# Halved span loads and 64x64 state products in a linear-attention plus gated-MLP kernel

## The chip, the cores and the metric

The kernel runs on one core of a Trainium2 chip. The core has a matrix engine (TensorE, in the profile PE, with its weight loads as PEld), a vector engine (VectorE, DVE), an activation engine (ScalarE, ACT), a general-purpose engine (GpSimd, POOL) and a queue engine (SyncE, SP) that issues DMA transfers. GpSimd issues DMA transfers too. The metric is the device time of one execution in microseconds; the median of three runs is 202.58 us (202.42 to 202.94).

## The reference, cut to what matters

Two stages are computed one after the other. The first is linear attention with a decay per head, in blocks of 64 positions; 4 batches, 8 heads, 768 positions, head size 64:

```
for b in range(12):
    intra = einsum('bhic,bhjc->bhij', qb, kb) * Dmask      # lam ** (i - j) for i >= j
    intra = einsum('bhij,bhjd->bhid', intra, vb)
    inter = einsum('bhid,bhde->bhie', qb * lam_pow, kv_state)
    out[block b] = intra + inter
    kv_state = lam_block * kv_state + einsum('bhsd,bhse->bhde', kb * rev_pow, vb)
```

The second is a gated MLP on the 3072 rows of 512 numbers that the attention gives: h = x @ w_in (512 to 2048), g = h * cos(h), result g @ w_out (2048 to 512). Inputs and result are float32; the matrix products of the kernel are in bfloat16.

## The kernel before, in words

The work is cut into 24 blocks of 128 positions, and these into MLP tiles of 4, 2, 2, 2, 2, 2, 2, 4 and 4 blocks. An MLP tile takes the transposed attention output xT, multiplies it by 16 column chunks of w_in (L732), turns each into g on ScalarE (cos, L738) and VectorE (product, L744), and multiplies g by w_out in groups of four chunks (L778). ScalarE copies the result out (L792), and SyncE stores it.

The first four blocks are two "spans" (`add_span`, x = 0 and 1) of 256 positions each, one for each of the first two batches. In a span a row of the tile holds two neighbouring positions. For each span SyncE loads q and k (512 KB each, all 8 heads at once), and GpSimd loads v. q and k are scaled by head halves hp = 0 and 1 (L593: VectorE, but GpSimd for k of the second span), transposed on TensorE (L601), copied by ScalarE (L604), multiplied to scores (L612) and masked on VectorE (L617). Then come the values (L638), the state of the span's first half (`update`, L625), its copies into kv_bd (L629), the part of the output that comes from that state (`carried`, L644), and the copies into xT (L652) from which the first MLP tile starts. In `update` a product takes two heads at once: 64 positions, a 128-wide k and a 128-wide v, so that of each 128x128 result only the two 64x64 blocks on the diagonal are used.

The later blocks are handled in pairs: `prepare` scales q (L329), k (L333) and v (L337) and transposes; `add_scores` and `add_stretch` compute scores, state and values in 64x64 products. For the first pair (blocks 4 and 5) the first q is scaled on VectorE and the second on GpSimd. From block 6 on the transposes are DMA transposes.

The order of the instructions on every engine is not written by hand. A small planner (`Planner.order`) plays the tasks through with a length, a latency and a priority for each, and gives the order in which they are issued. So a changed length or latency in the code moves other instructions too. Where the plan leaves TensorE without work in the lead-in, `keep_awake` puts in filler matmuls (L866, L870) of the planned length.

The loads stand in a list of their own: `ORDER` (L36) gives the first ones, and the loop at L817 the dependencies. The first pair's q waits for the MLP's first tile to be nearly through its gate (`pace`), v4 waits for k4 to have landed, and the last quarter of w_out (o3) waits for q4. Chunks of w_in and w_out are converted to bfloat16 by the DMA, issued on GpSimd.

Of the kernel before, what the change touches and what calls it, by code (L numbers as in the profile page):

```python
# [18 lines left out]
SPANS = 2  # L19
# [6 lines left out]
LOAD_US = 1.22  # L26
# [118 lines left out]
def kernel(  # L145
# [10 lines left out]
    nc = tc.nc  # L156
    B, H, S, D = q.shape
    P = 128
# [68 lines left out]
    pl = Planner({**BUFS, "q_f": BUFS["ld"], "k_f": BUFS["ld"], "v_f": BUFS["ld"]})  # L227
# [3 lines left out]
    halves = [slice(i * D, (i + 1) * D) for i in range(2)]  # L231
# [9 lines left out]
    load_t, issue_t = {}, {}  # L241
# [15 lines left out]
        return i  # L257

    def add_span_load(name, src, x, prio, deps):
        def emit(_):  # L260
            if on_pool:
                t = span_v[x]
            else:
                if ("raw", x) not in live:
                    live["raw", x] = work.tile([P, 2, H, 2, D], F32, tag="g", name="sp_f")
                t = live[name, "sp", x] = live["raw", x][:, "qk".index(name[0])]
            return start(nc.gpsimd if on_pool else nc.sync, t.rearrange("u h s d -> u h (s d)"),
                         src[x, :, 0:2 * P, :].rearrange("h (u s) d -> u h (s d)", s=2), deps)

        on_pool = name == "v_f"  # L270
        issue, load_t[name, "sp", x] = dma("POOL" if on_pool else "SP", 1.5, 1.0 if on_pool else 0.5, emit, prio, deps,
                                           lat=0.95 if on_pool else 1.0)
        return load_t[name, "sp", x]

    def add_load(n, name, src, prio, deps=()):
        b, c = where(n)

        def emit(_):
            t = loads.tile([P, H, D], F32, tag=name, name=name)
            live[name, n] = t  # L280
            i = start(nc.sync, t, src[b, :, c * P:(c + 1) * P, :].transpose([1, 0, 2]), deps)
            if (name, n) == ("q_f", 2 * SPANS):

                tc.add_manual_dep(i.ins, pace[0].ins.ins.name, mybir.DependencyInfo(
                    mybir.DependencyClass.Sync, mybir.DependencyReason.DATA), reason="order of loads")
            return i

        issue_t[name, n], load_t[name, n] = dma("SP", LOAD_US, 0.85, emit, prio, deps, get=name,
                                                lat=1.9 if name == "v_f" and n < 2 * SPANS + 2 else 1.0)
        return load_t[name, n]  # L290

    w_t, pace = {}, []
# [22 lines left out]
    def prepare(pr):  # L315
# [24 lines left out]
        a, k_ = [], []  # L340
        for s in range(2):
            n = 2 * pr + s
            eq = "DVE" if early and s == 0 else "POOL"
            ev = "DVE" if early and s == 1 else "POOL"
            a.append(pl.add(eq, us[eq], [load_t["q_f", n]] + a, partial(prep_q, s=s, e=eq), pa(-0.9), get=None if s else "qk"))
            k_.append(pl.add("ACT" if early else "POOL", 0.61, [load_t["k_f", n]] + ([] if early else [a[0]]), partial(prep_k, s=s), pa(-0.9)))
            d_t[n] = v_head[n] = pl.add(ev, us[ev], [load_t["v_f", n]], partial(prep_v, s=s, e=ev), pa(-0.85), get="v_s")
            for name, t in (("q_f", a[s]), ("k_f", k_[s]), ("v_f", d_t[n])):
                issue_t[name, n].frees = [t]
# [229 lines left out]
    def add_span(x):  # L579
# [40 lines left out]
        def update(t):  # L620
            L["kv"] = bank(t.bank[0], [P, NP, P], F32, "ps_kv")
            rows = chunks[0][0]
            for p in range(NP):
                for s in range(2):
                    nc.tensor.matmul(L["kv"][:, p, :], lhsT=L["k"][rows, s, 2 * p:2 * p + 2, :], rhs=L["v"][rows, s, 2 * p:2 * p + 2, :],  # L625
                                     start=(p == 0 and s == 0), stop=True, skip_group_check=True)

        def update_out(_, h, e):
            (nc.scalar.copy if e == "ACT" else nc.vector.tensor_copy)(kv_bd[h, x, :, h], L["kv"][h, :, h])  # L629
# [23 lines left out]
                live["xT", 0][:, :, n * P:(n + 1) * P], L["o"][c])  # L653

        s_first = None
        so, kt, v_t = [[], []], [], [load_t["v_f", "sp", x]]
        for hp in range(2):
            eq, ek = QK[x]["q"][hp], QK[x]["k"][hp]
            a = pl.add(eq, us[eq], [load_t["q_f", "sp", x]], partial(prep, name="q", hp=hp, e=eq), pa(-0.9 + 0.1 * hp))
            kt.append(pl.add(ek, us[ek], [load_t["k_f", "sp", x]], partial(prep, name="k", hp=hp, e=ek), pa(-0.9 + 0.1 * hp)))  # L660
            if x:
                w_t["in", 2].issue.deps.append(kt[hp])
            outs = []
            for name, src in (("qT", a), ("kT", kt[hp])):
                e = OUTS[x][name][hp]
                t = pl.add("PE", MM(P, 4), [src, s_first if name == "kT" else None], partial(transposes, name=name, hp=hp), pa(-0.5 + 0.1 * hp), banks=1)
                outs.append(pl.add(e, 0.58 if e == "ACT" else 0.42, [t], partial(transposes_out, name=name, hp=hp, e=e), pa(-0.5 + 0.1 * hp)))
                t.bank_frees = [[outs[-1]]]
            s1 = pl.add("PE", 0.42, outs, partial(scores, hp=hp), pa(0.1 + 0.1 * hp), banks=2)
            if x and hp == 0:  # L670
                s_first = s1
            so[hp] = [pl.add("DVE", 0.69, [s1], partial(scores_out, hp=hp, i=i), pa(0.1 + 0.1 * hp + 0.05 * i)) for i in range(2)]
            s1.bank_frees = [[t] for t in so[hp]]

        u = pl.add("PE", 0.42, v_t + kt + [spans[0].get("carried")], update, pv(0.1), banks=1)
        Uo_sp[x] = [pl.add(e, 0.4 if e == "ACT" else 0.42, [u], partial(update_out, h=h, e=e), pv(0.1))
                    for h, e in zip(halves, STATE_OUT[x])]
        u.bank_frees = [Uo_sp[x]]
        span_deps.extend(v_t + kt)
        v0 = pl.add("PE", 0.35, so[0] + v_t + [spans[0].get("carried")], partial(values, hp=0), pv(0.2), banks=2)  # L680
        v1 = pl.add("PE", 0.35, [v0] + so[1], partial(values, hp=1), pv(0.25))
# [249 lines left out]
```

## Time and profile before

| what | value |
|---|---|
| median of 3 runs | 202.58 us |
| the profiled execution's own time | 202.54 us |
| span of its instructions | 200.8 us |
| TensorE busy | 195.9 us (98%) |
| VectorE, ScalarE, GpSimd busy | 116.3, 119.4, 64.9 us |
| TensorE clock granted | 0.998 |
| q, k, v loads of a pair, median to landing | 3.9, 4.2, 5.1 us |

The span counts from the first to the last profiled instruction; the execution's own time is 1.7 us longer. A busy time of TensorE counts waiting inside its pipeline too, so 98% doesn't say that it is at its peak. Times in the timeline are from the span's start. A group's line gives the engine, the kernel line, what is written and read, and how often.

### The profile page before, as it was taken

How to read it: one execution, taken by the hardware profiler on the slowest of the kernel's cores; microseconds unless marked ns; L12 is line 12 of the kernel's file. 1: busy time of each engine (PE TensorE's matmuls, PEld its weight loads, DVE VectorE, ACT ScalarE, POOL GpSimd, SP SyncE). 2: the span in 40 equal slices, each digit the busy share in tenths (PEclk: the TensorE clock that was granted, in tenths of full speed). 3: DMA queues.
4: the chain of work that ended last, by engine and by line, in shares of the span. 5: the costliest groups of instructions: out<-in, count | busy, mean ns of one | idle time of the engine just before them, and what ended most of it. 6: DMA issues, size and time to landing. Idle time of an engine off the chain costs nothing.

```text
span 200.8 us, 5951 instructions
## 1 busy us (share of the span) xinstructions
PE 195.9 (98%) x2473; PEld 116.8 (58%) x2473; DVE 116.3 (58%) x230; ACT 119.4 (59%) x241; POOL 64.9 (32%) x85
## 2 busy tenths in 40 slices
PE   6999999999999999999999999999999999999994
PEld 3477444558757757766658676755445544444452
DVE  3978771269756948758458575835588354444001
ACT  4878771149658768666639666644887564345120
POOL 5893003085235360635555353545500000000000
PEclk9999999999999999999999999999999999999999
DMA  5999999999889997999999899979910010111112
GB/s 163 303 190 204 203 199 216 209 238 225 200 197 225 262 202 177 239 179 253 189 275 245 188 207 194 277 141 261 243 23 3 3 52 0 52 55 52 52 52 104
DMA packets 96620, 33.93 MB, mean 169 GB/s; under 512 B 84690, under 2 KB 93650, under 8 KB 96594
## 3 DMA queue, kind: packets, MB, share of 16 engines
q1 hardware_dynamic: 89088, 28.78, 63.2%
q0 software_dynamic: 7360, 4.72, 16.4%
q8 instruction: 19, 0.31, 0.7%
q10 hardware_dynamic: 146, 0.07, 0.1%
q14 instruction: 7, 0.06, 0.1%
HBM read 27.26 MB, written 6.29 MB: 167 GB/s over the span
## 4 chain that ended last, share of the span: by engine, by line
PE 95%; DMA 2%; ACT 0%; DVE 0%; SPq 0%; issue 0%; ACTq 0%; DVEq 0%
PE ps_h L732 42%; PE ps_f L778 42%; DMA sp_f<-in_k_dram 2%; PE ps_s L407 2%; PE ps_o L502 2%; PE ps_o L470 2%; PE ps_kv L419 1%; PE ps_t L601 1%; PE ps_s L612 1%; PE ps_o L638 1%; PE ps_kv L625 1%; PE ps_x L470 0%; PE ps_idle L870 0%; PE ps_t L359 0%; DVE k_sp L593 0%; PE ps_o L644 0%
## 5 line engine op out<-in xcount | busy, mean ns | idle before, releaser
L744 DVE TENSOR_TENSOR g<-ps_h,cos 128x256 bf16<-128x256 f32 (+1 forms) x149 | 73.1, 501 | 42.0 <-ACT cos L738 41.1
L738 ACT ACTIVATE cos<-ps_h,halfpi 128x256 f32<-128x256 f32 (+1 forms) x149 | 75.9, 536 | 29.3 <-PE ps_h L732 28.2
L778 PE MATMUL ps_f<-w_out_sb,g 128*128 128x512 bf16 (+2 forms) x400 | 91.4, 371 | 0.0
L732 PE MATMUL ps_h<-xT,w_in_sb 128*128 128x256 bf16 (+1 forms) x596 | 91.1, 303 | 0.0
L732 PEld LDWEIGHTS <-w_in_sb 128*128 128x128 bf16 x596 | 57.5, 98 | 30.1 <-DVE xT L510 0.4
L778 PEld LDWEIGHTS <-g 128*128 128x128 bf16 x400 | 37.6, 98 | 37.2
L329 POOL TENSOR_TENSOR qk<-q_f,q_scale 128x512 bf16<-128x512 f32 x19 | 20.0, 1067 | 34.7 <-DMA q_f<-in_q_dram 17.6
L792 ACT COPY o_sb<-ps_f 128x512 f32<-128x512 f32 (+1 forms) x24 | 13.7, 572 | 24.7 <-PE ps_f L778 24.5
L337 POOL TENSOR_TENSOR v_s<-v_f,v_scale 128x512 bf16<-128x512 f32 x19 | 19.6, 1042 | 9.8 <-DMA v_f<-in_v_dram 5.2
L412 DVE TENSOR_TENSOR s_m<-ps_s,mask 128x512 bf16<-128x512 f32 x20 | 13.0, 685 | 4.2 <-PE ps_s L407 3.6
L333 POOL CAST qk<-k_f 128x512 bf16<-128x512 f32 x18 | 11.0, 611 | 10.4 <-DMA k_f<-in_k_dram 10.2
L510 ACT CAST xT<-ps_o 128x512 bf16<-128x512 f32 x11 | 6.0, 588 | 9.0 <-PE ps_o L502 5.6
L425 DVE TENSOR_TENSOR sum<-sum,ps_kv 128x512 f32<-128x512 f32 x15 | 10.2, 682 | 0.6
L430 ACT CAST S<-sum 128x512 bf16<-128x512 f32 x15 | 9.1, 616 | 0.9 <-DVE sum L425 0.8
L253 POOL DMA_DIRECT2D w_out_sb<-in_moe_w_out_dram x4 | 3.0, 784 | 15.8 <-DMA q_f<-in_q_dram 15.8
L792 DVE COPY o_sb<-ps_f 128x384 f32<-128x384 f32 x1 | 0.6, 557 | 11.6 <-DMA out_dram<-o_sb 11.6
L470 PEld LDWEIGHTS <-v_s 64*64 64x64 bf16 x320 | 4.0, 107 | 4.2 <-issue 3.4
L870 PE MATMUL ps_idle<-blank 128*128 128x512 f32 (+2 forms) x8 | 4.7, 707 | 1.7 <-DVE blank L215 1.7
L487 DVE COPY spare<-ps_o 1x1 f32<-1x1 f32 x6 | 0.9, 156 | 8.4 <-PE ps_o L470 8.4
L617 DVE TENSOR_TENSOR s_m_sp<-ps_s,mask_sp 128x512 bf16<-128x512 f32 x8 | 5.1, 684 | 1.2 <-PE ps_s L612 1.2
L470 PE MATMUL ps_o<-s_m,v_s 64*64 64x64 bf16 x256 | 5.2, 196 | 0.0
L502 PE MATMUL ps_o<-qkT,S 64*64 64x64 bf16 x304 | 4.9, 195 | 0.0
(76 smaller groups left out, 90.1 us busy)
## 6 DMA issues: line engine op xcount, KB each, us to landing
q_f<-in_q_dram SPq DMA_DIRECT2D x20, 256.0 KB, 3.9
k_f<-in_k_dram SPq DMA_DIRECT2D x20, 256.0 KB, 4.2
v_f<-in_v_dram SPq DMA_DIRECT2D x20, 256.0 KB, 5.1
out_dram<-o_sb SPq DMA_DIRECT2D x19, 256.0 KB, 2.5
w_out_sb<-in_moe_w_out_dram POOLq DMA_DIRECT2D x4, 512.0 KB, 12.4
sp_f<-in_q_dram SPq DMA_DIRECT2D x2, 512.0 KB, 4.9
sp_f<-in_k_dram SPq DMA_DIRECT2D x2, 512.0 KB, 5.5
w_in_sb<-in_moe_w_in_dram POOLq DMA_DIRECT2D x2, 512.0 KB, 8.9
```

Of the source, the lines that this page charges most:

```text
L329: vec[e].tensor_mul(new_qk()[:, 0, :, s], live.pop(("q_f", 2 * pr + s)), q_scale[:, c, :].unsqueeze(2).to_broadcast([P, H, D]))
L333: (nc.scalar.copy if early else nc.gpsimd.tensor_copy)(new_qk()[:, 1, :, s], live.pop(("k_f", 2 * pr + s)))
L337: vec[e].tensor_mul(live["v_s", 2 * pr + s], live.pop(("v_f", 2 * pr + s)), v_scale[:, c, :].unsqueeze(2).to_broadcast([P, H, D]))
L412: nc.vector.tensor_mul(t, live["s", pr][s], mask.unsqueeze(1).to_broadcast([P, H, D]))
L425: nc.vector.tensor_add(new, live["sum", pr, 0] if half else live["sum", pr - 1, 1], live["kv", pr][half])
L430: nc.scalar.copy(new_S(pr, half), live["sum", pr, half])
L470: yield lambda h=h: nc.tensor.matmul(o[halves[h % 2], h // 2], lhsT=live["v_s", n0 + s][m, h, :], rhs=live["s_m", n0 + s][m, h, :], start= ...
L732: nc.tensor.matmul(t[:, :n], lhsT=w_in_sb[:, kd, f * P:(f + 1) * P], rhs=live["xT", i][:, kd, at], start=(kd == 0), stop=(kd == KD - 1))
L738: nc.scalar.activation(c[:, :n], live["h", i, f, at.start][:, :n], AF.Sin, bias=halfpi)
L744: return nc.vector.tensor_mul(live["g", i][:, f, at], live.pop(("h", i, f, at.start))[:, :n], live.pop(("c", i, f, at.start))[:, :n])
L778: nc.tensor.matmul(live["f", i, j, piece][:, :width], lhsT=live["g", i][:, f, j * P:(j + 1) * P], rhs=w_out_sb[:, f, part], start=(f == 0) ...
L792: (nc.scalar.copy if eng == "ACT" else nc.vector.tensor_copy)(o[:, :width], live["f", i, j, piece][:, :width])
```

## The change

- `add_span_load` issues the load of a span's q or k as two loads, one for each half of the heads, each planned at half the length and with a latency of 0.7 us where it was 1.0. The scaling of a head half depends on its own half alone. v is loaded whole as before.
- In the plan, the first pair's loads get 1.0 us each (they had 1.22), and their v a latency of 2.7 us (it had 1.9). v4 no longer depends on the landing of k4.
- The first pair's second q is scaled on VectorE.
- `update` of a span makes its state in 16 products on 64x64 blocks where it had 8 on 64x128, two heads' blocks for each head pair and each of the two positions of a row.
- The planned lengths of a span's scores, update and values are changed to 0.32, 0.3 and 0.3 us.

The planner's order on all engines follows from these numbers. The built order differs in the lead-in on TensorE, ScalarE and VectorE, in SyncE's queue of loads, stores and DMA transposes, and in the places where small attention products stand between the MLP's groups.

```
     def add_span_load(name, src, x, prio, deps):
-        def emit(_):
+        on_pool = name == "v_f"
+        cuts = [slice(0, H)] if on_pool else [slice(0, H // 2), slice(H // 2, H)]
+
+        def emit(_, cut):
...
-            return start(nc.gpsimd if on_pool else nc.sync, t.rearrange("u h s d -> u h (s d)"),
-                         src[x, :, 0:2 * P, :].rearrange("h (u s) d -> u h (s d)", s=2), deps)
...
-        issue, load_t[name, "sp", x] = dma("POOL" if on_pool else "SP", 1.5, 1.0 if on_pool else 0.5, emit, prio, deps,
-                                           lat=0.95 if on_pool else 1.0)
-        return load_t[name, "sp", x]
+            return start(nc.gpsimd if on_pool else nc.sync, t[:, cut].rearrange("u h s d -> u h (s d)"),
+                         src[x, cut, 0:2 * P, :].rearrange("h (u s) d -> u h (s d)", s=2), deps)
+
+        parts = [dma("POOL" if on_pool else "SP", 1.5 / len(cuts), 1.0 if on_pool else 0.5, partial(emit, cut=cut), prio, deps,
+                     lat=0.95 if on_pool else 0.7)[1] for cut in cuts]
+        load_t[name, "sp", x] = parts if len(parts) > 1 else 2 * parts
+        return parts[-1]
...
-        issue_t[name, n], load_t[name, n] = dma("SP", LOAD_US, 0.85, emit, prio, deps, get=name,
-                                                lat=1.9 if name == "v_f" and n < 2 * SPANS + 2 else 1.0)
+        issue_t[name, n], load_t[name, n] = dma("SP", 1.0 if n < 2 * SPANS + 2 else LOAD_US, 0.85, emit, prio, deps, get=name,
+                                                lat=2.7 if name == "v_f" and n < 2 * SPANS + 2 else 1.0)
...
-            eq = "DVE" if early and s == 0 else "POOL"
+            eq = "DVE" if early else "POOL"
...
-                    nc.tensor.matmul(L["kv"][:, p, :], lhsT=L["k"][rows, s, 2 * p:2 * p + 2, :], rhs=L["v"][rows, s, 2 * p:2 * p + 2, :],
-                                     start=(p == 0 and s == 0), stop=True, skip_group_check=True)
+                    for i, h in enumerate(halves):
+                        nc.tensor.matmul(L["kv"][h, p, h], lhsT=L["k"][rows, s, 2 * p + i, :], rhs=L["v"][rows, s, 2 * p + i, :],
+                                         start=(p == 0 and s == 0), stop=True, skip_group_check=True)
...
-            a = pl.add(eq, us[eq], [load_t["q_f", "sp", x]], partial(prep, name="q", hp=hp, e=eq), pa(-0.9 + 0.1 * hp))
-            kt.append(pl.add(ek, us[ek], [load_t["k_f", "sp", x]], partial(prep, name="k", hp=hp, e=ek), pa(-0.9 + 0.1 * hp)))
+            a = pl.add(eq, us[eq], [load_t["q_f", "sp", x][hp]], partial(prep, name="q", hp=hp, e=eq), pa(-0.9 + 0.1 * hp))
+            kt.append(pl.add(ek, us[ek], [load_t["k_f", "sp", x][hp]], partial(prep, name="k", hp=hp, e=ek), pa(-0.9 + 0.1 * hp)))
...
-            s1 = pl.add("PE", 0.42, outs, partial(scores, hp=hp), pa(0.1 + 0.1 * hp), banks=2)
+            s1 = pl.add("PE", 0.32, outs, partial(scores, hp=hp), pa(0.1 + 0.1 * hp), banks=2)
...
-        u = pl.add("PE", 0.42, v_t + kt + [spans[0].get("carried")], update, pv(0.1), banks=1)
+        u = pl.add("PE", 0.3, v_t + kt + [spans[0].get("carried")], update, pv(0.1), banks=1)
...
-        if name == f"v{2 * SPANS}":
-            deps = [load_t["k_f", 2 * SPANS]]
+        if name in (f"v{2 * SPANS}", f"v{2 * SPANS + 1}"):
+            deps = []
```

More of the change, by code (lines that the diff above doesn't have):

```diff
@@ L266, in emit @@
                 t = live[name, "sp", x] = live["raw", x][:, "qk".index(name[0])]
-            return start(nc.gpsimd if on_pool else nc.sync, t.rearrange("u h s d -> u h (s d)"),
-                         src[x, :, 0:2 * P, :].rearrange("h (u s) d -> u h (s d)", s=2), deps)
-        on_pool = name == "v_f"
-        issue, load_t[name, "sp", x] = dma("POOL" if on_pool else "SP", 1.5, 1.0 if on_pool else 0.5, emit, prio, deps,
-                                           lat=0.95 if on_pool else 1.0)
-        return load_t[name, "sp", x]
+            return start(nc.gpsimd if on_pool else nc.sync, t[:, cut].rearrange("u h s d -> u h (s d)"),
[4 more added lines that the diff above has]
+        return parts[-1]
     def add_load(n, name, src, prio, deps=()):
@@ L655, in add_span @@
         s_first = None
-        so, kt, v_t = [[], []], [], [load_t["v_f", "sp", x]]
+        so, kt, v_t = [[], []], [], [load_t["v_f", "sp", x][0]]
         for hp in range(2):
             eq, ek = QK[x]["q"][hp], QK[x]["k"][hp]
-            a = pl.add(eq, us[eq], [load_t["q_f", "sp", x]], partial(prep, name="q", hp=hp, e=eq), pa(-0.9 + 0.1 * hp))
-            kt.append(pl.add(ek, us[ek], [load_t["k_f", "sp", x]], partial(prep, name="k", hp=hp, e=ek), pa(-0.9 + 0.1 * hp)))
+            a = pl.add(eq, us[eq], [load_t["q_f", "sp", x][hp]], partial(prep, name="q", hp=hp, e=eq), pa(-0.9 + 0.1 * hp))
+            kt.append(pl.add(ek, us[ek], [load_t["k_f", "sp", x][hp]], partial(prep, name="k", hp=hp, e=ek), pa(-0.9 + 0.1 * hp)))
             if x:
@@ L679, in add_span @@
         span_deps.extend(v_t + kt)
-        v0 = pl.add("PE", 0.35, so[0] + v_t + [spans[0].get("carried")], partial(values, hp=0), pv(0.2), banks=2)
-        v1 = pl.add("PE", 0.35, [v0] + so[1], partial(values, hp=1), pv(0.25))
+        v0 = pl.add("PE", 0.3, so[0] + v_t + [spans[0].get("carried")], partial(values, hp=0), pv(0.2), banks=2)
+        v1 = pl.add("PE", 0.3, [v0] + so[1], partial(values, hp=1), pv(0.25))
         second = pl.add("PE", MM(P, 4) + 0.1, [v1] + Uo_sp[x], carried, pv(0.3))
```

## The prediction

> **What bounds the kernel now.** I read the busy shares first, then the chain that ended last, then the first 17 us in order of time, then the DMA. On the page, the first line is busy time per engine, the second the chain's shares:
>
> ```profile
> PE 195.9 (98%) x2473; PEld 116.8 (58%) x2473; DVE 116.3 (58%) x230; ACT 119.4 (59%) x241; POOL 64.9 (32%) x85
> ...
> PE 95%; DMA 2%; ACT 0%; DVE 0%; SPq 0%; issue 0%; ACTq 0%; DVEq 0%
> ```
>
> TensorE is the chain. In the costliest groups its matmuls L732 and L778 show 0.0 us idle, so from the first gate matmul to the end there is no gap to win; only the lead-in can move the end earlier. The timeline of the lead-in (start, length, engine, work):
>
> ```profile
> 9.47 2.04 POOL L593 TENSOR_TENSOR k_sp<-sp_f,k_sp 128x512 bf16<-128x512 f32 x2 [0.96 <-DMA sp_f<-in_k_dram]
> ...
> 10.57 0.40 PE L601 MATMUL ps_t<-ident,k_sp 128*128 128x128 bf16 x4
> ...
> 10.90 0.62 PE L625 MATMUL ps_kv<-v_sp,k_sp 64*128 64x128 bf16 x8
> ...
> 11.45 0.42 PE L638 MATMUL ps_o<-s_m_sp,v_sp 64*64 64x128 bf16 x16
> ...
> 11.55 0.74 ACT L629 CAST kv_bd<-ps_kv 64x256 bf16<-64x256 f32 x2
> ...
> 12.70 0.40 PE L644 MATMUL ps_o<-qT_sp,kv_bd 128*128 128x128 bf16 x4
> ...
> 12.93 1.08 ACT L652 CAST xT<-ps_o 128x512 bf16<-128x512 f32 x2
> ...
> 14.14 1.48 PE L732 MATMUL ps_h<-xT,w_in_sb 128*128 128x256 bf16 x12
> ...
> 15.91 0.40 PE L644 MATMUL ps_o<-qT_sp,kv_bd 128*128 128x128 bf16 x4
> ...
> 16.69 7.27 PEld L732 LDWEIGHTS <-w_in_sb 128*128 128x128 bf16 x47 [0.23 <-DMA w_in_sb<-in_moe_w_in_dram]
> ```
>
> The second span's k lands at 9.30, GpSimd starts 0.17 later and delivers at 10.51; from 10.57 TensorE never stops. The last line is a second limit: at 16.69 TensorE waits for the third w_in chunk (column block f=4), issued at 11.46. DMA issues in that window (KB, us to landing), then the stretches (last two columns: DMA share, GB/s):
>
> ```profile
> w_in_sb<-in_moe_w_in_dram POOLq DMA_DIRECT2D x1, 128.0 KB, 5.2
> ```
> ```profile
> 2.00:3.00 1.00, 1.00 (x2) 0.15 (x1) 0.27 (x2) 0.65 (x1) 0.89 (x3) 1.00 0.58 126
> 3.00:4.00 1.00, 1.00 (x4) 0.96 (x4) 0.07 (x1) 0.18 (x1) 0.54 (x3) 1.00 1.08 328
> 9.00:11.00 2.00, 1.98 (x28) 0.96 (x25) 2.00 (x5) 1.16 (x2) 1.53 (x2) 1.00 1.83 182
> 12.00:14.00 2.00, 2.00 (x72) 1.58 (x64) 1.29 (x2) 1.84 (x5) 2.00 (x4) 1.00 1.45 197
> 16.00:20.00 4.00, 4.00 (x34) 2.90 (x34) 3.21 (x8) 3.36 (x8) 0.72 (x1) 1.00 1.26 205
> ```
>
> The f=4 chunk landed at 11.46+5.2 = 16.65 and was used 0.05 us later. The DMA engines are full from 3 us on; v and the weights pass at 182 to 205 GB/s without a pause, so their landings are set by bytes queued ahead.
>
> **What the Trainium skill says.** "DMA: Bandwidth & Descriptors", Rules for kernel authors, says of two transfers to disjoint partition halves not to bother, since both spray over the same DMA engines and serialize. Here the cut is by heads, but the point is the same, and the trace agrees: four 512 KB loads land at 4.7, 6.2, 7.8 and 9.3, one per 1.5 us. A half lands earlier; the second half doesn't. "TensorEngine Tiling (Array Packing)", Tiling Modes, says that 64x64 gives four independent tiles and 64x128 two, and that a mode change drains the array. The trace agrees: sixteen 64x64 products (L638) start 0.24 to 0.35 us before what follows, eight 64x128 (L625) 0.55.
>
> **The change, part by part.**
> *Halves of q and k.* SyncE issues eight loads for four. The four issues took 0.45 to 1.50 us, the last ending at 4.78; the later ones wait on drained traffic, so I price the extra issues at nothing: the data behind them covers it. If not, each costs at most the shortest, 0.45. Landings from the 0.75 us per half: first q half 3.95, first k half 5.5 (not 6.2), second span's first k half 8.55 (not 9.30), last k half still 9.3. Opening q starts no earlier: TensorE's fillers run to 5.6. GpSimd's first k product runs 8.72 to 9.76 (1.04 each in the 2.04 row), the second ends at 10.76 (was 11.51). So 0.75 us is won there. The v and weight loads follow the same bytes: nothing, and TensorE used f=4 only 0.05 us after its landing, so nothing beyond 0.05 us survives f=4 unless the bytes move.
>
> *Update as 16 products.* The nearest row is L697, 32 products of 128x64 in 0.62 us in the chain: 16 take 0.31. Lower bound 0.24 (L638 spacing), upper 0.55 (no gain). I take 0.31, 0.24 saved, twice.
>
> *The new order on TensorE.* The planner's costs changed, and the built order of instructions shows what it made of them. Before, after the second span's first k transpose: update, values, scores, k transpose, values, carried. After: a 448-column f32 filler, scores, second k transpose, update, both values, second q transpose, filler, carried. ScalarE gets both k copies before the state copies, and a q copy between those and xT. With spacings (start to next start) from the timeline: transpose 9.82 (+0.24), filler 10.06 (512 columns took up to 1.08 at 9.47; two passes of 0.49 shortened to 448 give 0.85), scores 10.91 (0.33), k transpose 11.24 (0.33), update 11.57 against 10.90 before. ScalarE: k copy 0.43 after its transpose, 11.67 to 12.25; state copies (0.74) to 12.97; q copy (0.58) to 13.5; carried 13.03 against 12.70; the xT pair (1.08, overlapping 0.05) to 14.53; first gate matmul 0.13 later as before (14.01 to 14.14): 14.66. So the gate starts 0.5 us later although k comes 0.75 earlier: the filler and scores put ahead of the update, and two 0.58 copies put ahead of xT, eat it.
>
> *From there to f=4.* Eight gate matmuls (0.87, mode change 0.10) to 15.63, values 0.35, carried 0.23: 16.21; f=2 and f=3, eight at 0.109: 17.08 for f=4 against 16.69. Its chunk has long landed. Loss 0.39, less what I can't resolve: 0.37. The order of f after that is the same, 400 L778 and 596 L732 matmuls in both, and 22 groups of small-tile work between them in both: no further difference.
>
> *First pair's v behind its k.* v4 (33.89) no longer waits for k4's landing (33.81), so v4 and v5 enter about 2 us earlier, ahead of the last w_out chunk (issued 32.55 when q4 lands, landed 6.6 later at 39.14, first used at about 41.3). *Second q on VectorE:* 0.69 us instead of 1.06 on GpSimd. VectorE was idle for 2.8 us after its first q (32.74 to 35.51): that hides it; uncovered it would cost 0.69. SyncE's queue is reordered: two row-interleaved stores now follow the first DMA transposes, others swap with loads. The transposes, issued from 48.06 to 50.8, landed by 52.3 for use at 54.7; they are now wanted some 3 us earlier (52 gate matmuls ahead of them, not 64 and 8 L778) and leave two stores (about 2 us) earlier: margin about 1 us, no cost.
>
> *Sum.* 202.54 of the profiled run (span 200.8 and 1.7 around it) + 0.37 = 202.91; against the median of 202.58 it is 202.95. I say 202.9.
>
> **The rivals.**
> *A, slower by more than 0.3%: the last w_out chunk comes late.* v4 and v5, issued just after it at 33.89 and 34.31, landed only at 40.1 and 41.0, after it, so the order of issue decides. Now two, perhaps three loads of 256 KB stand ahead, at about 1 us each: landing 39.14+0.37+2 to 3 = 41.5 to 42.5, first use 41.3+0.37 = 41.7. Over 2.2 us of traffic ahead, it decides: stall up to 0.8, time 203.3 to 203.8. Against: the idle ramp before the chunk (147 GB/s in 34 to 37) would be filled. The skill's same DMA page (Queues, rings and completion order) says that each DMA engine goes round the queues packet by packet, which would soften it; v4's landing after the chunk shows little of it.
> *B, faster: loads start flowing sooner.* DMA ran at 126 GB/s in 2 to 3 us and 328 in the next. If short transfers fill that second, up to 0.6 us of traffic moves forward, and v, w_in and w_out with it: the gate at about 14.1, f=4 at 16.5: 202.2, at the very best 201.9. Nothing in the trace says why the first second is slow.
> *C, no change:* landings suit the new order better than I reckon, the filler ends before k arrives, the gate starts at 14.1, and f=4's landing holds TensorE at 16.69 as before: 202.5 to 202.6.
>
> **How the numbers follow.** My case 0.45 (own range 202.6 to 203.2), A 0.25, B 0.13, C 0.17. About 0.3% (0.6 us) is what a measurement tells from no change: 201.97 to 203.19 is "same". Faster: the extreme of B, 0.07. Slower: A, 0.23, and the top of my case, 0.05: 0.28. Same 0.65. The range, 202.2 to 203.7, leaves out B's best and A's worst.
>
> **What would show it.** Second span's first k product on GpSimd starts at 8.7; update row L625 becomes 16 products with 0.3 to the next; first gate matmul at 14.6; no wait for w_in at f=4; L778 and L732 still without idle time. A gate start before 14.0 with f=4 used before 16.5 proves B; a wait of L778 for w_out near 41.7 proves A. I am wrong if TensorE shows other new gaps after 17 us, since I found none to expect.

## The result, and the profile after

The changed kernel is slower: 210.15 us (median of 6 runs, 206.66 to 212.29) against 202.72 us for the kernel before (6 runs, 202.42 to 203.51); the ratio is 1.0251, 95% interval 1.0215 to 1.0287. The forecast was 202.9, with a range to 203.7. Executions of one kernel scatter, so ratios are taken from those within 1.5% of its fastest; the profiled execution of the changed kernel, 210.44 us, is one of its slower ones, and its numbers below are an upper case. A milder loss is shown by the first experiment, profiled at 206.06 us.

From the page, busy time per engine and the shares of the chain that ended last:

```profile
PE 196.7 (94%) x2464; PEld 119.0 (57%) x2492; DVE 116.8 (56%) x231; ACT 119.6 (57%) x241; POOL 63.8 (31%) x84
...
PE 69%; DMA 15%; SPq 10%; issue 2%; POOL 1%; ACT 1%; DVE 1%; POOLq 0%; ACTq 0%
```

TensorE is busy about as long as before (196.7 us for 195.9), but its share of the chain went from 95% to 69%: 25% are now DMA and SyncE's queue. (A share of the chain isn't time lost: TensorE has other work beside most of it.) These pieces of the chain lie where TensorE had to wait (start, length, what):

```profile
5.58 7.54 DMA sp_f<-in_k_dram
...
55.05 2.75 DMA qkT<-qk
57.84 0.45 PE ps_s L410 x32
```

Two places: the last half of the second span's k, issued at 5.58, takes 7.54 us to 13.12; and DMA transposes arrive late for the scores at 57.84, and again at 85.08 and 96.66. The timeline of the lead-in, to be held against the lines shown of before (what was L593, L601, L625, L732 is now L596, L604, L629, L736):

```profile
10.07 1.04 POOL L596 TENSOR_TENSOR k_sp<-sp_f,k_sp 128x512 bf16<-128x512 f32 x1 [1.89 <-DMA sp_f<-in_k_dram]
13.19 1.04 POOL L596 TENSOR_TENSOR k_sp<-sp_f,k_sp 128x512 bf16<-128x512 f32 x1 [2.08 <-DMA sp_f<-in_k_dram]
```
```profile
11.17 0.40 PE L604 MATMUL ps_t<-ident,k_sp 128*128 128x128 bf16 x4 [1.01 <-POOL k_sp L596]
...
14.29 0.61 PE L604 MATMUL ps_t<-ident,k_sp 128*128 128x128 bf16 x4 [1.57 <-POOL k_sp L596]
...
19.46 1.57 PE L736 MATMUL ps_h<-xT,w_in_sb 128*128 128x256 bf16 x8
...
34.53 1.67 PE L782 MATMUL ps_f<-w_out_sb,g 128*128 128x512 bf16 x7
```

The first w_out matmul before:

```profile
28.82 6.21 PE L778 MATMUL ps_f<-w_out_sb,g 128*128 128x512 bf16 x28
```

GpSimd's second k product starts at 13.19; the forecast had 9.76. The first gate matmul follows at 19.46 (14.14 before), the first w_out matmul at 34.53 (28.82 before): 5.7 us of the span's 7.9 (208.7 for 200.8). The order on TensorE is the one the prediction read from the built kernel; its start is what moved.

Stretches of the lead-in (length, busy time and count for PE, PEld, DVE, ACT, POOL, then TensorE's clock, DMA share, GB/s):

```profile
2.00:3.00 1.00, 1.00 (x2) 0.15 (x1) 0.27 (x2) 0.65 (x1) 0.89 (x3) 1.00 0.64 189
4.00:5.00 1.00, 1.00 (x2) 0.38 (x2) 0.84 (x3) 0.85 (x5) 0.27 (x1) 1.00 0.75 150
9.00:11.00 2.00, 0.99 (x22) 0.54 (x21) 2.00 (x5) 1.15 (x2) 0.93 (x1) 1.00 1.49 211
13.00:15.00 2.00, 0.71 (x10) 0.52 (x12) 1.05 (x2) 0.07 (x1) 1.81 (x3) 0.68 1.42 187
15.00:17.00 2.00, 2.00 (x53) 1.63 (x52) 0.00 (x0) 1.34 (x4) 2.00 (x3) 0.50 1.18 131
```

Three things stand here. The microsecond from 2 to 3 carries more than before (189 GB/s for 126), as rival B hoped, but the one from 4 to 5 falls to 150, where the kernel before moved 348. TensorE is busy for 0.99 us of the two from 9 to 11 and 0.71 of those from 13 to 15, where before it was busy almost throughout. And its clock falls: by the trace it is 1.00 until 13.71, half of that until 20.54, then 1.00 again. So the clock fell after k had landed (13.12) and is not what made k late, but what follows the late k runs at half speed: four transposes take 0.61 us at 14.29 and took 0.40 at 11.17. The Trainium skill describes such a fall in "TensorE: Matmul & The Clock Gate", Part 1, What's actually happening: after an idle window of about 3.4 us the array gets half of its clock pulses. The trace agrees in the size, 0.50, but shows no idle window of that length: the pause of TensorE in which the clock fell lasted 1.57 us (12.72 to 14.29), and none around it was longer.

The list of waits over the whole execution (us in total, times, longest):

```profile
POOL k_sp L596 <- DMA sp_f<-in_k_dram: 4.0, 2, 2.1
PEld L410 <- DMA qkT<-qk: 2.9, 4, 1.3
PE ps_s L410 <- DMA qkT<-qk: 1.6, 3, 0.8
```

The two lines with qkT are new: before, no engine waited for a DMA transpose. TensorE's own 1.6 us of them are most of what the trace shows for the other part of the loss: from the start of its first w_out matmul to that of its last the changed kernel takes 170.8 us (34.53 to 205.34), the kernel before 168.9 (28.82 to 197.70).

### The profile page after: what moved, and what is told of

It is laid out like the page before. It is cut to its first block, busy times and chain, and to the rows that moved or that the text cites. A ratio compares the mean times of both kernels' runs of the same rounds, so it can differ in the third digit from the quotient of the medians.

```text
span 208.7 us, 5968 instructions
## 1 busy us (share of the span) xinstructions
PE 196.7 (94%) x2464; PEld 119.0 (57%) x2492; DVE 116.8 (56%) x231; ACT 119.6 (57%) x241; POOL 63.8 (31%) x84
## 3 DMA queue, kind: packets, MB, share of 16 engines
HBM read 27.26 MB, written 6.29 MB: 161 GB/s over the span
## 4 chain that ended last, share of the span: by engine, by line
PE 69%; DMA 15%; SPq 10%; issue 2%; POOL 1%; ACT 1%; DVE 1%; POOLq 0%; ACTq 0%
PE ps_h L736 33%; PE ps_f L782 29%; SPq L253 10%; DMA qkT<-qk 6%; DMA v_f<-in_v_dram 5%; DMA sp_f<-in_k_dram 4%; PE ps_s L410 1%; PE ps_o L505 1%; PE ps_kv L422 1%; PE ps_o L473 1%; PE ps_o L642 1%; POOL v_s L340 1%; ACT cos L742 1%; PE ps_t L604 1%; DVE g L748 1%
## 5 line engine op out<-in xcount | busy, mean ns | idle before, releaser
L736 PE MATMUL ps_h<-xT,w_in_sb 128*128 128x256 bf16 (+1 forms) x592 | 92.6, 304 | 0.2
L782 PE MATMUL ps_f<-w_out_sb,g 128*128 128x512 bf16 (+2 forms) x376 | 88.9, 370 | 2.5 <-issue 1.7
L736 PEld LDWEIGHTS <-w_in_sb 128*128 128x128 bf16 x596 | 58.1, 98 | 31.8 <-DVE xT L513 0.4
L332 POOL TENSOR_TENSOR qk<-q_f,q_scale 128x512 bf16<-128x512 f32 x18 | 18.6, 1042 | 32.2 <-DMA q_f<-in_q_dram 22.4
L874 PE MATMUL ps_idle<-blank 128*128 128x320 f32 (+3 forms) x8 | 4.9, 738 | 1.7 <-DVE blank L215 1.7
L410 PE MATMUL ps_s<-qkT 64*64 64x64 bf16 x320 | 4.4, 194 | 1.6 <-DMA qkT<-qk 1.6
L607 ACT COPY kT_sp<-ps_t 128x512 bf16<-128x512 bf16 x4 | 2.3, 586 | 4.9 <-PE ps_t L604 4.9
```

Of the source, the lines that this page charges most:

```text
L332: vec[e].tensor_mul(new_qk()[:, 0, :, s], live.pop(("q_f", 2 * pr + s)), q_scale[:, c, :].unsqueeze(2).to_broadcast([P, H, D]))
L736: nc.tensor.matmul(t[:, :n], lhsT=w_in_sb[:, kd, f * P:(f + 1) * P], rhs=live["xT", i][:, kd, at], start=(kd == 0), stop=(kd == KD - 1))
L782: nc.tensor.matmul(live["f", i, j, piece][:, :width], lhsT=live["g", i][:, f, j * P:(j + 1) * P], rhs=w_out_sb[:, f, part], start=(f == 0) ...
```

## The experiments

My theory after the result: k is late because GpSimd's v loads are issued ahead of SyncE's last k half. The rivals: short loads are slow in themselves; or the other edits and the new order make the loss. The runs are grouped by question; each is timed against the kernel before on the same chip, which took 202.80, 202.92 and 203.15 us (medians of 23, 39 and 20 runs) in the three groups.

### The halves alone, and everything but the halves

In the kernel before, only `add_span_load` and the dependencies on the two halves are changed; the spans' planned scores and update, the first pair and the products stay. The core of it:

```
+        cuts = [slice(0, H)] if on_pool else [slice(0, H // 2), slice(H // 2, H)]
...
-            a = pl.add(eq, us[eq], [load_t["q_f", "sp", x]], partial(prep, name="q", hp=hp, e=eq), pa(-0.9 + 0.1 * hp))
+            a = pl.add(eq, us[eq], [load_t["q_f", "sp", x][hp]], partial(prep, name="q", hp=hp, e=eq), pa(-0.9 + 0.1 * hp))
```

> The kernel before with the q and k span loads halved and nothing else (the plan follows the halves). Theory 1, issue order: each half takes SyncE about 0.5 us to issue, so the last k half is issued at about 5.6, after GpSimd's v loads (4.7), and has to share the DMA engines with v and w_in: it lands at 12 to 13 instead of 9.3, and the gate starts 3 us or more later: 206 to 210. Theory 2, the rest of the change does it (v4 ungated, the new order, late DMA transposes): about 203, last k half at 9.5. Theory 3, short loads lower the DMA rate as such: k lands late too, but v does not land before it.

Measured: 208.54 us (4 runs, 206.06 to 211.39), ratio 1.021 (1.0121 to 1.0299). GpSimd's timeline:

```profile
4.71 1.96 POOL L253 DMA_DIRECT2D v_sp<-in_v_dram  x2 [1.05 <-DMA sp_f<-in_q_dram]
...
10.12 1.04 POOL L596 TENSOR_TENSOR k_sp<-sp_f,k_sp 128x512 bf16<-128x512 f32 x1 [1.95 <-DMA sp_f<-in_k_dram]
12.37 1.04 POOL L596 TENSOR_TENSOR k_sp<-sp_f,k_sp 128x512 bf16<-128x512 f32 x1 [1.21 <-DMA sp_f<-in_k_dram]
```

The halving alone makes k late: its second half is used at 12.37, the gate starts at 16.48. It is enough for nearly all of the loss (ratio 1.021, where the change has 1.0251). Between theory 1 and theory 3 it doesn't decide by the sign that I had named: v lands at 12.41, just behind k. The runs that move v do.

The other way round, the changed kernel with q and k loaded whole:

```
-        cuts = [slice(0, H)] if on_pool else [slice(0, H // 2), slice(H // 2, H)]
+        cuts = [slice(0, H)]
...
-                     lat=0.95 if on_pool else 0.7)[1] for cut in cuts]
+                     lat=0.95 if on_pool else 1.0)[1] for cut in cuts]
```

> The kernel after with whole span loads again, all else of the change kept. Theory 1 (issue order): the last k lands at 9.3, the gate starts at 13.9 to 14.3, 202 to 204. Theory 2 (the rest of the change): 205 or more. In both, what is above 202.7 is the price of the other parts, waits of the scores for DMA transposes among them.

Measured: 203.98 us (20 runs), ratio 1.0059 (1.0036 to 1.0082). k lands at 9.45, the gate starts at 14.19, no scores wait for a transpose. The planner makes another order here than in the changed kernel. So 1.2 us of loss are left without any halving; part of it in this execution is a pause of TensorE of 0.68 us near 16.7, put down to "issue" (more on it below).

### When v is issued

GpSimd's first v load waits for q: in the kernel before for the whole first q (landed at 4.75), in the changed one for the second half of it (4.43). The last issues of k and the first of v, before:

```profile
3.28 1.50 SPq L253 DMA_DIRECT2D sp_f<-in_k_dram  x1
5.05 1.96 POOL L253 DMA_DIRECT2D v_sp<-in_v_dram  x2 [1.39 <-DMA sp_f<-in_q_dram]
```

and in the changed kernel:

```profile
4.21 2.12 SPq L253 DMA_DIRECT2D sp_f<-in_k_dram  x2
4.73 1.96 POOL L253 DMA_DIRECT2D v_sp<-in_v_dram  x2 [1.07 <-DMA sp_f<-in_q_dram]
```

So the halves do two things to the order of issue: SyncE, which needs eight issues, ends its last one at 6.33 instead of 4.78; and v starts at 4.73 instead of 5.05. v, once behind all of q and k, now goes in ahead of the last half of k. Three runs move v. First, in the changed kernel, v behind the first span's second k half:

```
-            kept.append(add_span_load(which + "_f", src[which], n, at - 2040, kept[0:1] if name == "v0" else []))
+            kept.append(add_span_load(which + "_f", src[which], n, at - 2040, kept[1:2] if name == "v0" else []))
```

> The kernel after, halves kept, but GpSimd's first v load waits for the first span's second k half (7.7) instead of its second q half (4.4), so that all eight halves are issued first. Theory 1: the last k half lands at 9.5 to 10.5 instead of 13.1; v lands at 12.5 to 13.5, so the gate starts at about 16.5 and the time is 204 to 207, better than the change by 2 us or more. Theory 3 (short loads slow the DMA as such): the last k half stays at 12 or later, and the time is 209 or more.

Measured: 208.04 us (4 runs), ratio 1.0239 (1.0179 to 1.0298). That is outside the 204 to 207 expected, and by the ratio no better than the changed kernel. Yet k's own delay is gone. v is issued at 7.30, and GpSimd's two k products then run back to back:

```profile
7.30 1.96 POOL L253 DMA_DIRECT2D v_sp<-in_v_dram  x2 [3.64 <-DMA sp_f<-in_k_dram]
...
10.82 2.49 POOL L596 TENSOR_TENSOR k_sp<-sp_f,k_sp 128x512 bf16<-128x512 f32 x2
```

k had landed before: nothing waits for its second half, and SyncE's last packet ran by 9.7 us. But GpSimd is held until 10.75 by the issues of v and two w_in chunks, which now come later. Its products start at 10.82 and 11.83 (10.07 and 13.19 in the changed kernel), the clock stays at 1.00, and the gate starts earlier than in the changed kernel (19.46), though later than before (14.14):

```profile
16.14 1.05 PE L736 MATMUL ps_h<-xT,w_in_sb 128*128 128x256 bf16 x8
```

The rest of its loss stands elsewhere. Of the 5.3 us by which its span is longer than that of the kernel before (206.1 for 200.8), 2.2 are there at the first w_out matmul (31.01 for 28.82); 3.1 come after it, where TensorE waits 1.6 us for DMA transposes. So the run shows that k comes in time once v is issued behind it, not that moving v mends the kernel.

Second, in the kernel before, with its whole loads, v with no dependency at all:

```
-            kept.append(add_span_load(which + "_f", src[which], n, at - 2040, kept[0:1] if name == "v0" else []))
+            kept.append(add_span_load(which + "_f", src[which], n, at - 2040, []))
```

> The kernel before, whole loads, but GpSimd's first v load is issued without waiting for q. Theory 1: v's descriptors (from about 3.7) get ahead of part of the second span's k (issued to 4.8), so k lands at 11 or later though no load is shorter, and the time is 204 to 208. Theory 3: k lands at 9.3 as before and the time is 202 to 203.

Measured: 203.45, 208.24, 208.65 and 211.26 us. The profile is of the last:

```profile
3.62 1.96 POOL L253 DMA_DIRECT2D v_sp<-in_v_dram  x2
12.45 2.04 POOL L593 TENSOR_TENSOR k_sp<-sp_f,k_sp 128x512 bf16<-128x512 f32 x2 [5.37 <-DMA sp_f<-in_k_dram]
```

Nothing is halved here, and k comes 3 us late (issued 3.30, landed 12.28), with TensorE's clock at 1.00 until 13.6 us. Among the loads only GpSimd's were moved, v and the w_in chunks behind it. One of the four executions was as fast as the kernel before; that k came in time there is likely, but it wasn't profiled.

Third, only the first span's loads are halved, which makes six (the second span's are planned with the latency of whole loads again):

```
-        cuts = [slice(0, H)] if on_pool else [slice(0, H // 2), slice(H // 2, H)]
+        cuts = [slice(0, H)] if on_pool or x else [slice(0, H // 2), slice(H // 2, H)]
```

> The kernel after, but only the first span's q and k are halved: six loads on SyncE, the second span's q and k whole. Issue order theory: the last k is issued from about 4.0, before GpSimd's first v load (4.7), and its 1024 packets are mostly in the queue by then: k lands at 9.5 to 10.5, gate at 14.5 to 15.5, time 203 to 206. If short loads harm by themselves, half of the harm (2 to 4 us) stays with k landing before v's.

Measured: 210.04 us (4 runs), ratio 1.0243 (1.0138 to 1.0349); k products from 12.35. The expectation missed: I thought that six issues would still be through before v. SyncE's last one runs from 3.49 to 5.25, v starts at 4.70.

### Halves, with v later

If the order of issue is the cause, halves must do little harm once v is issued behind them without holding GpSimd too long. In the halves-only kernel, v waits for the first span's first k half:

```
+        first_half[name, x] = parts[0]
...
-            kept.append(add_span_load(which + "_f", src[which], n, at - 2040, kept[0:1] if name == "v0" else []))
+            kept.append(add_span_load(which + "_f", src[which], n, at - 2040, [first_half["k_f", 0]] if name == "v0" else []))
```

> The kernel before with the halved q and k loads alone, and GpSimd's first v load waiting for the first span's first k half (which landed at 6.3 in the changed kernel) where it waited for the second q half. Nothing else. Theory 1 (order of issue: k is late because v, 1 MB over both spans, is issued at 4.7, ahead of the second span's last k half at 5.6): v is now issued at about 6.4, when the last k half has left SyncE; that half lands at 10 at the latest, v0 at 11.5 to 12.3, the gate starts near 15, time 203.5 to 205, at least 3 us under the 208.5 of the halves with v at 4.7. Theory 2 (six or eight short loads are slow as such, whatever stands beside them): k still at 12 or later, 207 to 209.

Measured: 205.29 us (12 runs, 203.82 to 208.1), ratio 1.0076 (1.0047 to 1.0106), where the halves alone had 1.0121 to 1.0299. That is a little above the 203.5 to 205 expected, but some 3 us came back by moving one issue from 4.71 to 6.29 (the planner's order on TensorE moved with it):

```profile
6.29 1.96 POOL L253 DMA_DIRECT2D v_sp<-in_v_dram  x2 [2.63 <-DMA sp_f<-in_k_dram]
...
9.82 2.56 POOL L597 TENSOR_TENSOR k_sp<-sp_f,k_sp 128x512 bf16<-128x512 f32 x2
```

k no longer waits for its DMA; the gate starts at 15.24. The rest is v and the weights, which now come later: v lands at 11.76 (10.72 before), and a gate matmul waits for its w_in chunk:

```profile
16.68 0.61 PE L736 MATMUL ps_h<-xT,w_in_sb 128*128 128x256 bf16 x4 [0.39 <-DMA w_in_sb<-in_moe_w_in_dram]
```

The same delay in the changed kernel with its first-pair edits undone (that kernel without the delay follows below):

```
-            kept.append(add_span_load(which + "_f", src[which], n, at - 2040, kept[0:1] if name == "v0" else []))
+            kept.append(add_span_load(which + "_f", src[which], n, at - 2040, [first_half["k_f", 0]] if name == "v0" else []))
```

> The changed kernel with the edits to the first pair undone (loads planned as before, v4 behind k4, second q on GpSimd), and GpSimd's first v load waiting for the first span's first k half as in the run beside it. Halves, 16 products and the span's planned lengths stay. Theory 1 (order of issue, with the late transposes following from the late lead-in together with the first pair's edits): last k half by 10, gate near 15, no wait of the scores for DMA transposes over 0.5, time 204 to 205.5, against 206.35 with v at 4.7. Theory 2: k at 12 or later, 206 to 207.

Measured: 205.86 us (4 runs), ratio 1.011 (1.0071 to 1.0149), against 1.0119 (1.0052 to 1.0185) without the delay: no difference that can be told. k's products start at 9.78, as theory 1 said, but v, issued at 6.26, lands at 13.12 and TensorE waits for it:

```profile
13.17 0.37 PE L630 MATMUL ps_kv<-v_sp,k_sp 64*64 64x64 bf16 x12 [1.68 <-DMA v_sp<-in_v_dram]
```

After that its clock falls to 0.50 in 15 to 17 us, and the gate starts at 18.03. (The profiled execution took 207.12 us.) Why v took 6.9 us here and 5.5 in the run above, issued at the same time, isn't settled.

### The first pair, the update and the order

The kernel before with the edits to the first pair's loads and its second q alone:

```
-            eq = "DVE" if early and s == 0 else "POOL"
+            eq = "DVE" if early else "POOL"
...
-        if name == f"v{2 * SPANS}":
-            deps = [load_t["k_f", 2 * SPANS]]
+        if name in (f"v{2 * SPANS}", f"v{2 * SPANS + 1}"):
+            deps = []
```

(and the planned 1.0 and 2.7 us of the loads).

> The kernel before with the first pair's edits alone: v4 free of k4, plan values 1.0 and 2.7 for its loads, second q on VectorE. The lead-in is as before, gate at 14.1. If these edits make the late DMA transposes, the scores wait 1 to 3 us for them and the time is 204 to 206; if those waits come from the late lead-in, none shows and the time is 202.5 to 203.2. v4, v5 and the last quarter of w_out land within 1 us of each other, at 38 to 42, in both.

Measured: 203.23 us (20 runs), ratio 1.001 (0.9989 to 1.0031): no difference. Rival A's wait is there, small:

```profile
PE ps_f L778 <- DMA w_out_sb<-in_moe_w_out_dram: 0.4, 1, 0.4
```

The last w_out chunk, issued at 32.64, landed at 41.82 (39.14 before).

The changed kernel with these edits undone (the planned times of the loads too):

```
-            eq = "DVE" if early else "POOL"
+            eq = "DVE" if early and s == 0 else "POOL"
...
-        if name in (f"v{2 * SPANS}", f"v{2 * SPANS + 1}"):
-            deps = []
+        if name == f"v{2 * SPANS}":
+            deps = [load_t["k_f", 2 * SPANS]]
```

> The kernel after with the first pair's edits undone. The last k half still lands at about 13 and the gate still starts at 17 or later. If the first pair's edits make the late transposes, the waits of the scores (2.9 us in the profile of the change) are gone and it is 2 to 3 us faster than the change: 204 to 208; if not, they stay, 207 to 211.

Measured: 206.35 us (4 runs), ratio 1.0119 (1.0052 to 1.0185). Weight loads of the scores wait 0.4 us for the transposes over the whole execution (2.9 in the changed kernel). Long waits of this kind, 2.3 to 3.0 us, stand only in the four profiles with both the first pair's edits and a late lead-in; elsewhere they are 0 to 1.0 us, and the 1.0 is in the kernel with the update alone, below, which has neither.

The kernel before with the 16 products alone, planned at 0.3:

```
-        u = pl.add("PE", 0.42, v_t + kt + [spans[0].get("carried")], update, pv(0.1), banks=1)
+        u = pl.add("PE", 0.3, v_t + kt + [spans[0].get("carried")], update, pv(0.1), banks=1)
```

(with the products of `update` as in the change).

> The kernel before with the state update as 16 products on 64x64 blocks, planned at 0.3, and nothing else. An update takes 0.24 to 0.31 us to the next start instead of 0.55, so the gate starts up to 0.5 earlier unless w_in's first chunk or ScalarE's copies hold it; the third w_in chunk lands at 16.65 as before and holds TensorE at column block 4: 202.4 to 202.9, no change beyond 0.3%. A gain of 0.4 us or more would show that this landing doesn't bind.

Measured: 203.68 us (20 runs), ratio 1.0025 (1.0004 to 1.0046): if anything a little slower. The products do start 0.19 to 0.27 us ahead of what follows (0.55 before), and the gate starts at 14.17, as before. There is a pause that the kernel before lacks:

```profile
17.01 0.33 PE L645 MATMUL ps_o<-qT_sp,kv_bd 128*128 128x128 bf16 x3 [0.68 <-issue]
```

Last, the order of instructions by itself: the changed kernel, planned as for halves, so that every engine has its order, but with each q and k loaded whole in the place of its first half.

```
+            if cut.start:
+                return whole[name, x]
-            return start(nc.gpsimd if on_pool else nc.sync, t[:, cut].rearrange("u h s d -> u h (s d)"),
-                         src[x, cut, 0:2 * P, :].rearrange("h (u s) d -> u h (s d)", s=2), deps)
+            whole[name, x] = start(nc.gpsimd if on_pool else nc.sync, t.rearrange("u h s d -> u h (s d)"),
+                                   src[x, :, 0:2 * P, :].rearrange("h (u s) d -> u h (s d)", s=2), deps)
+            return whole[name, x]
```

> The changed kernel with its own order of instructions on every engine, planned as for halves, but each q and k of a span is loaded whole at the place of its first half, and nothing is loaded at the place of the second. So the instruction order that the prediction priced at +0.37 us runs with whole loads. If the prediction's price of the order is right and only the loads were wrong: last k lands near 9.4, gate at 14.2 to 14.8, time 202.9 to 204.0 (up to 0.7 of it the pause of TensorE near 16.8 that two kernels with 16 products showed). If the order itself is costly, the gate is past 15.5 or TensorE waits 2 us and more for DMA transposes, and the time is 205 or more.

Measured: 205.04 us (9 runs), ratio 1.0085 (1.0057 to 1.0112). The loads are those of the kernel before (k at 9.34, v at 10.76, the w_in chunk of f=4 at 16.72), and still the gate is 1.25 us later:

```profile
9.51 2.04 POOL L600 TENSOR_TENSOR k_sp<-sp_f,k_sp 128x512 bf16<-128x512 f32 x2 [0.95 <-DMA sp_f<-in_k_dram]
```
```profile
15.39 1.03 PE L740 MATMUL ps_h<-xT,w_in_sb 128*128 128x256 bf16 x8
...
29.93 1.24 PE L786 MATMUL ps_f<-w_out_sb,g 128*128 128x512 bf16 x5
```

My expectation for this run, 14.2 to 14.8, was careless: the prediction's 14.66 rested on a first k product at 8.72, and whole loads give 9.51. The same steps from 9.51 give 14.66 + 0.79 = 15.45; measured is 15.39. Up to the gate the order costs what the prediction worked out for it, if the time of k is put in. By the sign named in the expectation (205 or more, or waits of 2 us) it is costly by itself. The waits for transposes are there too, with all loads in time:

```profile
PEld L414 <- DMA qkT<-qk: 2.3, 3, 1.3
```

## Why the prediction was wrong

**The step that failed** is that of the halves: "I price the extra issues at nothing: the data behind them covers it", and with it "last k half still 9.3" and "The v and weight loads follow the same bytes: nothing". The prediction took landings as set by the bytes queued ahead, and the queue as one. It is two: SyncE's and GpSimd's, each issued by its own engine, and from 8.23 us on packets of both run side by side in the changed kernel. Set side by side, the end of SyncE's last q or k issue, the start of GpSimd's first v issue, and the starts of GpSimd's two k products (of the first alone where they run as a pair, back to back):

| kernel | SyncE's last issue ends | v starts | k product |
|---|---|---|---|
| before | 4.78 | 5.05 | 9.47, 10.47 |
| all but the halves | 4.93 | 5.22 | 9.62, 10.63 |
| changed, v behind the second k half | 6.22 | 7.30 | 10.82 (pair), held by GpSimd's own issues |
| halves, v later | 5.97 | 6.29 | 9.82 (pair) |
| changed, first pair undone, v later | 6.06 | 6.26 | 9.78 (pair) |
| v at once, whole loads | 4.75 | 3.62 | 12.45 (pair) |
| first span's halves | 5.25 | 4.70 | 12.35 (pair) |
| halves alone | 6.56 | 4.71 | 10.12, 12.37 |
| changed, first pair undone | 6.25 | 4.75 | 10.06, 12.11 |
| changed | 6.33 | 4.73 | 10.07, 13.19 |

Where v's issue starts after SyncE is through, the last k product is at most 1.4 us late and does not wait for its data; where it starts before, it is 1.6 to 3 us late. The three kernels not in the table (first pair alone, update alone, order alone) have v 0.28 us after SyncE's last issue, and k in time. Two pairs of rows differ, as far as the loads go, only in when GpSimd's start (v and the w_in chunks behind it), one in each direction: v at once against before, and v later against the halves alone. The prediction noticed that SyncE's later issues were drawn out by traffic that had to drain (1.31 and 1.50 us) and used it as cover, but didn't ask who else issues in that time. The extra issues cost 1.55 us of SyncE's time (6.33 for 4.78), within its fallback of 0.45 each, and the event that lets v go comes 0.32 earlier; the margin was 0.27 us.

How v then stretches the tail of k is shown only in part. In the trace's list of packets, SyncE's last packet ran 0.5 us after GpSimd's first in the kernel before, and 3 to 5 us after it in the five kernels with k late. When GpSimd's first packet ran (8.47 us before, 8.23 in the changed kernel), 82 KB of SyncE's 2 MB were still to be moved before, 435 KB in the changed kernel and 593 KB with v at once. The Trainium skill's "DMA: Bandwidth & Descriptors", Queues, rings and completion order, says that a DMA engine goes round its queues packet by packet; the prediction cited that sentence for rival A and did not apply it to k and v. The stretched tail agrees with it. But the amount left doesn't decide alone: with the first span's halves and with halves and v later it was the same 179 KB, GpSimd's first packet ran at 8.57 and 8.43, and SyncE's last at 11.8 and 9.9. In the table these two differ in whether v's issue started before SyncE's last one had ended (4.70 for 5.25, 6.29 for 5.97). Why that matters so much stays open.

**The halves' gain.** The second span's first k half was to land at 8.55 and be used at 8.72. In the changed kernel it landed at 9.90 and was used at 10.07, though GpSimd was free from 8.19. With v delayed k is in time, but then GpSimd is in its issues until 9.8. So in none of the runs is the 0.75 us won.

**The order on TensorE** was right: +0.52 at the gate for k at 8.72, which with k at 9.51 is the 15.39 measured. Its further loss, 0.39 at f=4, fits: the first w_out matmul of the order-alone run is 1.11 us late (29.93 for 28.82), by the prediction's steps 0.39 + 0.79 = 1.18. The prediction's sum counted on the halves to pay 0.79 of it back. They didn't. About 1.1 us is what the order costs up to there with k as before; with k late by more it need not add in full.

**The clock.** From the second k product's start to the gate the prediction has 4.90 us (9.76 to 14.66); the changed kernel took 6.27 (13.19 to 19.46). The 1.37 more, over which the clock stood at 0.50 to 0.68, is a cost that the prediction had no term for. The order-alone run has the same order with the clock at 1.00 and takes 4.87 (10.52 to 15.39), so the fall of the clock is enough to account for it. With 3.43 us of late k, it makes the gate's 4.80 us beyond the forecast. How much idling it takes isn't settled: from 10.0 us on TensorE was busy 1.71 of 3.7 us in the changed kernel, with pauses of up to 1.57 us, and 1.71 of 3.5 with the first span's halves, with one of 1.61; the former lost half of its clock, the latter kept it.

**The transposes.** "margin about 1 us, no cost" failed. The prediction had them wanted 3 us earlier, and leaving 2 us earlier. In the order-alone run the scores stand 37.5 us after the gate's start (52.9 less 15.39; before 40.6), so the first held; but the two transposes leave 33.1 and 34.6 us after it (48.49 and 50.00), against 33.9 and 35.4 before: 0.8 us earlier, not 2. The second landed at 52.81 for scores at 52.9, with no margin left there, and scores at 68.00 and 80.50 wait 0.38 and 0.85 us. Two stores fewer do stand ahead of them, as counted; but SyncE's first store of that stretch itself leaves 30.8 us after the gate's start (46.16), before 30.3 (44.40). Counting the instructions ahead didn't tell when SyncE gets to them. The waits for transposes are not all that is lost this late: from the first w_out matmul to the end of the span the kernel before takes 172.0 us, the order-alone run 173.6, and the kernel with the first span's halves 175.4, with 1.7 us of TensorE's waits for transposes in it. The rest isn't accounted for here.

**The rivals.** Rival B's first half was right (189 GB/s instead of 126 between 2 and 3 us), but the microsecond from 4 to 5 gave it back. Rival A's mechanism exists and costs 0.4 us of wait at most where it could be seen alone, with no measurable change in time. Rival C didn't occur. None of the rivals had k late: the forecast had no case for the loss that came.

**What was right otherwise:** the update's spacing, nearly (0.31 forecast, 0.19 to 0.27 measured); that the first pair's edits alone change nothing in the time; and that the forecast would be wrong "if TensorE shows other new gaps after 17 us", which it does at 57.84 and after.

**Not settled.** In the stretch from 4 to 5 us the halved kernels move 150 to 283 GB/s (changed 150, halves alone 164, with v later 260, first span's halves 283), those with whole loads about 340 (before 348, order alone 339). It puts SyncE's data behind (1.5 MB moved by 7.99 us in the changed kernel, by 7.20 before) and widens the overlap with v. The first span's k shows it before any packet of v has run: its halves landed at 6.30 and 7.73 in the changed kernel, where the forecast had 5.5 for the first and the whole load landed at 6.24; with halves and v later they landed at 5.99 and 6.75. So short loads may cost something in themselves; no run separates it.

## What to carry to other kernels

When a load is split, look not only at its bytes but at who issues next to it: the added issues lengthen the issuing engine's time, and an event that came with the whole load may now come sooner and let another queue in. In these thirteen kernels no k load was late where its last issue had ended before the competing queue's first issue began; read both times and their margin (here 0.27 us) before pricing an issue at nothing. And an order planned on an early landing has a price of its own if that landing doesn't come.

## What the runs showed of the hardware

- SyncE's issue takes nearly the same for 256 KB as for 512 KB while nothing is in its way: 0.45 to 0.51 us for each of the first five halves, 0.45 and 0.57 for the first two whole loads. With more queued it is drawn out, to 1.33 us for one half in the changed kernel.
- Where v's issue falls into SyncE's, times spread: the kernel with v at once ran in 203.45 to 211.26 us over four executions, the kernel before in 202.54 to 204.89 over 23 on the same chip.
- Moving v's first issue from 4.71 to 6.29 us moved GpSimd's first packet only from 7.95 to 8.43.
- TensorE's clock fell to 0.50 with no pause longer than 1.57 us before it (changed kernel), and stayed at 1.00 after one of 1.61 (first span's halves).
- In two kernels with 16 products TensorE paused 0.68 us near 17 us with no wait behind it; the order-alone run, which has these products too, shows no such pause. The cause is open.
